# Key-side sums of linear attention: exponentials as the stationary operand, values with a column of ones as the moving one

## The chip, the cores and the metric

The kernel runs on one core of a Trainium2 chip. The metric is the device time of one execution in microseconds (us); the time before is the median of three runs, 832.02 us (829.52, 832.53 and 832.02). One further execution was recorded by the hardware profiler, and all rows below are from it.

The engines are named as the profile names them: PE is TensorE's matmul, PEld its weight load (the load of the stationary operand), DVE is VectorE, ACT is ScalarE, POOL is GpSimd and SP is SyncE, which issues nearly all DMAs here.

## The reference

Three stages follow each other. The first is linear attention over 4 batches, 8 heads, 576 tokens and head size 64; the change is in this stage alone.

```
proj = x @ w_phi                               # x is q or k, 64 -> 128 features
proj = proj - max(|proj|, over features)
phi(x) = [exp(proj), exp(-proj)]               # 256 features
kv  = sum over keys of phi(k)[f] * v[d]        # 256 x 64 per head
z   = sum over keys of phi(k)[f]               # 256 per head
out = (phi(q) @ kv) / (phi(q) @ z + 1e-6)
```

The second stage routes each token to one of 8 experts (two layers, 512 to 1024 to 512, with relu), the third is a gated feed-forward block with an RMS norm (512 to 1536 to 512). Their matmuls run in float32r, those of the attention in float32.

## The kernel before

The instructions are not written in the order in which they run. The code hands tasks to a planner (class `Graph`): each task has an engine, an estimated duration, its input and output buffers and a priority. The planner fills the engines' queues greedily: of the tasks whose inputs and buffers are there, it takes for an engine the one that can start first, and among equals the one with the lower priority number. The result is one fixed list for each engine, run in order.

For a batch b the function `attn` makes these tasks. Heads go in pairs; 512 of the 576 tokens ("main") are worked on pair by pair in four chunks of 128 (index c), and the 64 left over of all heads together (the pass "L"). The key passes come in the order pair 0, "L", pairs 1 to 3, with priorities b·100 + 0 to 4, the query passes after them from b·100 + 10 on. The experts' tasks of the batch have priorities from 1000 on, so they fill what the attention leaves.

- A pass loads its tokens (L417, L420), projects them on PE (L446, eight matmuls into one of two double banks named pq), takes the largest absolute value (L450, DVE) and subtracts it (L452, DVE, tile d). A bank is free again when the subtraction has read it.
- For keys, ACT makes both exponentials (L546, tile e; L539 for the left tokens, tile el).
- `kv_part` (L518) sums over the keys: the stationary operand is v of a chunk and head (128 keys x 64), the moving one both exponentials (128 keys x 256). The result lies with the 64 value columns on partitions, one head in each half of the partitions, ten matmuls a pair of heads (five chunks, the left tokens being the fifth).
- `sums` (L486) adds the exponentials of the chunks on DVE (L493; in batches 1 to 3 also L496 and L500), and `zn` (L504) finishes z on PE by matmuls with one moving column of ones (L515). In batch 0 there are 20 such matmuls a pair, in batches 1 to 3 eight.
- The sum over keys lies transposed to what the queries need. ACT copies it out of PSUM (L558, tile ks), and `ktr` (L561) has PE transpose both halves (L565) into the same bank beside z. DVE copies the bank out (L568, tile kv, 128 features x 2 heads x 2 halves x 65: 64 columns of kv and one of z).
- For queries, PE transposes d (L464, shown as L227), ACT makes the exponentials (L467, tile qp), and L613 multiplies: per head 16 matmuls of a stationary 128 x 64 (64 query tokens) with a moving 128 x 65 (kv and z). L580 does this for the left tokens. L475 to L479 divide on DVE; transposes and L624/L626 make the experts' input xh.

The host lays q, k and the left tokens out (`kernel`), v comes as it is.

Of the kernel before, what the change touches and what calls it, by code (L numbers as in the profile page):

```python
# [8 lines left out]
F32 = mybir.dt.float32  # L9
# [9 lines left out]
FE = 128  # L19
# [227 lines left out]
def dve(n, psum=False):  # L247
    return 0.13 + n / 960.0
# [6 lines left out]
class K:  # L255
# [123 lines left out]
    def attn_slots(self, ctx):  # L379
        g, p = self.g, self.pool(ctx, "at", side="left")  # L380
        self.attn_consts(p)
        mk = lambda *a: self.mk(p, *a)
        mk("qk", 6, [P, NC, P])
        mk("v", 3, [P, 2, NC, D])
        mk("vl", 2, [P, 2, NC, D])
        mk("d", 3, [P, 2, NC, FE])
        mk("e", 2, [P, 2 * NC, 2, FE])
        mk("el", 1, [P, NC, 2, FE])
        for _, _, a in g.slots["vl"]:
            self.nc.gpsimd.memset(a, 0.0)  # L390
        mk("es", 2, [P, 4, 2 * FE])
        mk("ks", 1, [P, 2 * FE])
        mk("qp", 2, [P, 2, NC, P])
        mk("qpl", 1, [P, 2, NC, P])
        mk("x", 2, [P, NC, P])
        mk("xl", 1, [P, 4 * D])
        mk("kv", 6, [P, 2, 2, D + 1])
        mk("m", 3, [P, 2 * NC])
        mk("r", 2, [P, NC])
        self.ones = p.tile([P, 1], F32, name="ones")  # L400
        self.nc.gpsimd.memset(self.ones, 1.0)
        self.halves = p.tile([P, 2], F32, name="halves")
        self.nc.gpsimd.memset(self.halves, 0.0)
        for j in range(2):
            self.nc.gpsimd.memset(self.halves[j * 64:j * 64 + 64, j:j + 1], 1.0)

    def attn(self, b, prio):

# [5 lines left out]
        def load(src, pr, np_):  # L414
            t = g.buf("qk")
            if pr != "L":
                g.t("SP", 0.5, lambda: nc.sync.dma_start(t.ap, src[b, pr].rearrange("p (c t) -> p c t", c=NC)),  # L417
                    w=[t], prio=np_, nbytes=2 * MAIN * D * 4)
            else:
                g.t(eng, 0.6, lambda: dma(t.ap, self.l[b].rearrange("p (c t) -> p c t", c=NC)),  # L420
                    w=[t], prio=-1 if b == 0 else np_, nbytes=2 * MAIN * D * 4)
            return t

        def load_v(pr, np_):
            if pr != "L":
                t = g.buf("v")
                g.t("SP", 0.5, lambda: nc.sync.dma_start(
                    t.ap, self.v[b, 2 * pr:2 * pr + 2, 0:MAIN].rearrange("h (p c) d -> p h c d", c=NC)),
                    w=[t], prio=np_ + (2.5 if b == 0 else 0), nbytes=2 * MAIN * D * 4)
                return t  # L430
            t = g.buf("vl")
            for j in range(2):
                g.t("SP", 0.6, lambda j=j: nc.sync.dma_start(
                    t.ap[j * 64:(j + 1) * 64, j], self.v[b, j::2, MAIN:S].rearrange("h t d -> t h d")),
                    w=[t], prio=np_ + (1.8 if b == 0 else 0), nbytes=LEFT * H * D * 2)
            return t

# [45 lines left out]
        kv, ready = {}, []  # L483
        el = vl = None

        def sums(pr, e, np_):  # L486


            es = g.buf("es")
            ev = lambda: e.ap.rearrange("p (j a k) f x -> p a j k (f x)", j=2, a=2)  # L490
            sv = lambda: es.ap.rearrange("p (j b) x -> p j b x", j=2)
            ex = lambda: el.ap[:, (pr % 2) * 2 + pr // 2].rearrange("p f x -> p (f x)")
            g.t("DVE", dve(1024), lambda: nc.vector.tensor_tensor(  # L493
                out=sv(), in0=ev()[:, 0], in1=ev()[:, 1], op=ALU.add), r=[e], w=[es], prio=np_)
            if b:
                g.t("DVE", dve(512), lambda: nc.vector.tensor_tensor(  # L496
                    out=sv()[:, :, 0], in0=sv()[:, :, 0], in1=sv()[:, :, 1], op=ALU.add), rw=[es], prio=np_)
                for j in range(2):
                    r = slice(j * 64, j * 64 + 64)
                    g.t("DVE", dve(256), lambda j=j, r=r: nc.vector.tensor_tensor(  # L500
                        out=sv()[r, j, 0], in0=sv()[r, j, 0], in1=ex()[r], op=ALU.add), r=[el], rw=[es], prio=np_)
            return es

        def zn(pr, es, pk):  # L504

            z = lambda x: pk.ap[x:x + 64, 0:4 * (D + 1)].rearrange("p (j f d) -> p j f d", j=2, f=2)[:, :, :, D]
            for f in range(2):
                todo = [] if b else [(lambda x, f=f: z(x)[:, :, f], el.ap[:, (pr % 2) * 2 + pr // 2, f], self.halves)]
                for j in range(2):
                    for i in range(1 if b else 2):  # L510
                        todo.append((lambda x, f=f, j=j: z(x)[:, j, f:f + 1], es.ap[:, 2 * j + i, f * FE:(f + 1) * FE],
                                     self.ones))
                for n, (o, w, m) in enumerate(todo):
                    for x in range(0, FE, 64):
                        nc.tensor.matmul(o(x), lhsT=w[:, x:x + 64], rhs=m, start=b > 0 or n == 0,  # L515
                                         stop=b > 0 or n == len(todo) - 1, skip_group_check=True)

        def kv_part(pr, e, v, np_, pk, part):  # L518


            def fn():
                for c in part:
                    for j in range(2):
                        v_, e_ = (v.ap[:, j, c], e.ap[:, j * NC + c]) if c < NC else (
                            vl.ap[:, j, pr], el.ap[:, (pr % 2) * 2 + pr // 2])
                        nc.tensor.matmul(pk.ap[j * 64:j * 64 + 64, 0:2 * FE], lhsT=v_,
                                         rhs=e_.rearrange("p f e -> p (f e)"), start=(c == 0), stop=(c == NC))
            g.t("PE", len(part) * 0.44 + 0.1, fn, r=([e, v] if 0 in part else []) + ([el, vl] if NC in part else []),
                rw=[pk], prio=np_)

        for i, pr in enumerate([0, "L", 1, 2, 3]):
            np_ = prio + i
            t = load(self.k, pr, np_)
            v = load_v(pr, np_)
            d = proj(t, np_)
            if pr == "L":
                el, vl, qpl = g.buf("el"), v, g.buf("qpl")
                for f in range(2):
                    g.t("ACT", act(512, False), lambda f=f, d=d: nc.scalar.activation(  # L539
                        el.ap[:, :, f].rearrange("p (h c) f -> p h c f", h=2), d.ap[:, :, 0:2], AF.Exp,  # L540
                        scale=1.0 - 2.0 * f), r=[d], w=[el], prio=np_)
                queries(d, lambda a, c: a[:, c % 2, 2 + c // 2], qpl, np_)
            else:
                e = g.buf("e")
                for f in range(2):
                    g.t("ACT", act(1024, False), lambda f=f, d=d, e=e: nc.scalar.activation(  # L546
                        e.ap[:, :, f], d.ap.rearrange("p h k f -> p (h k) f"), AF.Exp, scale=1.0 - 2.0 * f),
                        r=[d], w=[e], prio=np_)
                ready.append((pr, e, v, np_))
            if el is None:  # L550
                first = g.buf("pa")
                kv_part(*ready[0], first, range(NC))
                continue
            for pr, e, v, np_ in ready:
                pk, ks = first if pr == 0 else g.buf("pa"), g.buf("ks")
                es = sums(pr, e, np_)
                kv_part(pr, e, v, np_, pk, (NC,) if pr == 0 else range(NC + 1))
                g.t("ACT", act(256), lambda pk=pk, ks=ks: nc.scalar.copy(ks.ap, pk.ap[:, 0:2 * FE]),  # L558
                    r=[pk], w=[ks], prio=np_)

                def ktr(pr=pr, es=es, ks=ks, pk=pk):  # L561
                    zn(pr, es, pk)
                    o = pk.ap[:, 0:4 * (D + 1)].rearrange("p (j f d) -> p f j d", j=2, f=2)
                    for f in range(2):
                        nc.tensor.transpose(o[:, f, :, 0:D], ks.ap[:, f * FE:(f + 1) * FE], self.ident)  # L565
                g.t("PE", (0.9 if b else 1.3), ktr, r=[ks, es, el], rw=[pk], prio=np_)
                kv[pr] = g.buf("kv")
                g.t("DVE", dve(4 * (D + 1)), lambda pk=pk, o=kv[pr]: nc.vector.tensor_copy(  # L568
                    o.ap.rearrange("p j f d -> p (j f d)"), pk.ap[:, 0:4 * (D + 1)]), r=[pk], w=[kv[pr]], prio=np_)
            ready = []  # L570
# [763 lines left out]
```

## Time and profile before

| | |
|---|---|
| time, median of three runs | 832.02 us |
| the profiled execution | 829.16 us, its span 827.5 us |
| PE busy | 810.1 us, 98% of the span |
| DVE, ACT busy | 588.2 us, 399.7 us |
| mean granted TensorE clock | 0.995 of full speed |

The span is cut into three parts. The attention and the experts share the engines until some 395 us (the attention's last matmul starts at 270.8 us). In the stretch before 395 us the decoding of the third stage's weights begins on DVE and ACT; from 396 us on the third stage runs, whose matmuls are the largest groups of the page. A float32 matmul shows as two records, so a count of 16 is eight matmuls. Records of PE overlap, since a matmul's end is that of its last result; what a group of them costs is therefore read from its start to the start of the next group.

### The profile page before, as it was taken

Reading aid. Unit: us, or ns where it says so; the run is one execution under the profiler, and the core shown is the slowest. Engines: PE = TensorE matmul, PEld = TensorE weight load, DVE = VectorE, ACT = ScalarE, POOL = GpSimd, SP = SyncE. Lnnn points to the kernel's source line nnn. Section 1 sums busy time; section 2 is a strip of 40 time slices with the busy share of each in tenths; the row PEclk is TensorE's granted clock in tenths of the full one; section 3 lists DMA queues with packets and bytes.
Section 4 is the critical chain, followed back from the end, with each engine's and each line's share of the span. In section 5 each row is a group of like instructions: output and inputs, shape, how many; then the busy total and the mean of one; then the engine's idle time right before and its main releaser. Section 6 shows DMA issues by size and latency. Waiting matters only on the chain.

```text
span 827.5 us, 15957 instructions
## 1 busy us (share of the span) xinstructions
PE 810.1 (98%) x6552; PEld 745.3 (90%) x6553; DVE 588.2 (71%) x1041; ACT 399.7 (48%) x685; POOL 3.0 (0%) x20
## 2 busy tenths in 40 slices
PE   7989999999999999999799999999999999999997
PEld 6878898898989999999798999999999999999996
DVE  6697787777885459996699948898777554565533
ACT  4364363336534165451667545567354444454522
POOL 1000000000000000000000000000000000000000
PEclk9999999999999999999999999999999999999999
DMA  7354325424302555786537334553132223314102
GB/s 210 86 179 166 85 77 192 132 80 147 113 28 66 196 195 172 236 280 214 169 143 227 129 114 163 186 181 127 58 102 104 73 104 115 115 58 127 39 1 77
DMA packets 74560, 108.91 MB, mean 132 GB/s; under 512 B 10352, under 2 KB 55536, under 8 KB 73968
## 3 DMA queue, kind: packets, MB, share of 16 engines
q1 hardware_dynamic: 74176, 107.48, 39.5%
q8 instruction: 54, 0.88, 0.4%
q10 hardware_dynamic: 304, 0.33, 0.1%
q14 instruction: 26, 0.21, 0.1%
HBM read 73.11 MB, written 34.68 MB: 130 GB/s over the span
## 4 chain that ended last, share of the span: by engine, by line
PE 47%; ACT 2%; DVE 1%; issue 1%; DMA 0%; DVEq 0%; ACTq 0%
PE pz L1055 30%; PE pz L1101 17%; ACT w L934 0%; ACT L1080 0%; ACT fk L1061 0%; DMA out<-row 0%; DVE a L1093 0%; ACT row L870 0%; PE pz L1018 0%; ACT fk L1080 0%; DVE fk L1065 0%; DVE z L876 0%; DVE z L879 0%; DVE yu L973 0%; DVE fk L1088 0%
## 5 line engine op out<-in xcount | busy, mean ns | idle before, releaser
L1055 PE MATMUL pz<-xa,xh 128*128 128x384 f32 x798 | 151.4, 340 | 2.8 <-ACT fk L1061 2.1
L1055 PEld LDWEIGHTS pz<-xa,xh 128*128 128x128 f32 x798 | 141.7, 189 | 8.0 <-ACT fk L1061 3.0
L1055 PE MATMUL pz<-xa,w 128*128 128x384 f32 x714 | 133.9, 338 | 0.6 <-ACT fk L1061 0.6
L1055 PEld LDWEIGHTS pz<-xa,w 128*128 128x128 f32 x714 | 126.4, 188 | 4.6 <-ACT fk L1061 0.9
L1061 ACT ACTIVATE fk<-pz 128x384 f32<-128x384 f32 x144 | 70.6, 490 | 119.9 <-PE pz L1055 119.4
L1065 DVE TENSOR_TENSOR fk<-pz,fk 128x384 f32<-128x384 f32 x108 | 60.0, 555 | 93.0 <-PE pz L1055 53.5
L1101 PE MATMUL pz<-xh,a 128*128 128x512 f32 x342 | 87.1, 392 | 0.0
L1101 PE MATMUL pz<-w,a 128*128 128x512 f32 x306 | 78.8, 393 | 0.8 <-ACT a L1091 0.5
L761 PE MATMUL ph<-xh,w 128*128 128x288 f32 x528 | 77.0, 298 | 0.0
L761 PEld LDWEIGHTS ph<-xh,w 128*128 128x128 f32 x528 | 71.4, 188 | 2.4 <-issue 1.5
L1101 PEld LDWEIGHTS pz<-xh,a 128*128 128x128 f32 x342 | 63.4, 188 | 10.0 <-DVE a L1093 0.2
L770 PE MATMUL ph<-h,w 128*128 128x288 f32 x480 | 67.9, 296 | 0.0
L1101 PEld LDWEIGHTS pz<-w,a 128*128 128x128 f32 x306 | 56.6, 188 | 10.2 <-ACT a L1091 0.9
L770 PEld LDWEIGHTS ph<-h,w 128*128 128x128 f32 x480 | 64.5, 188 | 0.7 <-issue 0.4
L791 ACT CAST w<-wr 128x1024 fp32r<-128x1024 f32 x32 | 33.6, 1049 | 51.8 <-PE ps L770 14.4
L450 DVE TENSOR_REDUCE m<-pq 128x8 f32<-128x1024 f32 x36 | 43.7, 1219 | 14.7 <-PE pq L446 14.5
L1091 ACT CAST a<-fk 128x768 fp32r<-128x768 f32 x36 | 30.1, 836 | 43.8 <-DVE fk L1088 43.5
L467 ACT ACTIVATE qp<-ps 128x512 f32<-128x512 f32 x64 | 34.3, 603 | 31.4 <-PE ps L227 27.2
L1093 DVE TENSOR_TENSOR a<-fk,a 128x768 fp32r<-128x768 f32 x36 | 34.4, 955 | 18.9 <-ACT a L1091 18.9
L792 DVE TENSOR_TENSOR w<-wr,w 128x1024 fp32r<-128x1024 f32 x32 | 39.1, 1223 | 11.2 <-ACT w L791 11.0
L446 PE MATMUL pq<-wraw,qk 64*128 64x128 f32 x576 | 42.5, 287 | 3.8 <-DVE d L452 3.6
L446 PEld LDWEIGHTS pq<-wraw,qk 64*128 64x128 f32 x576 | 35.7, 190 | 9.1 <-DVE d L452 4.1
(190 smaller groups left out, 1168.7 us busy)
## 6 DMA issues: line engine op xcount, KB each, us to landing
wr<-in_moe_w SPq DMA_DIRECT2D x32, 512.0 KB, 3.7
z<-wdr SPq DMA_DIRECT2D x13, 896.0 KB, 4.6
xdr<-xh SPq DMA_DIRECT2D x4, 2304.0 KB, 8.7
wdr<-z SPq DMA_DIRECT2D x10, 896.0 KB, 4.6
yu<-ydr SPq DMA_DIRECT2D x8, 768.0 KB, 4.9
raw<-in_moe_w_val SPq DMA_DIRECT2D x12, 512.0 KB, 4.3
raw<-in_moe_w_gate SPq DMA_DIRECT2D x12, 512.0 KB, 4.5
raw<-in_moe_w_out SPq DMA_DIRECT2D x12, 512.0 KB, 3.9
```

Of the source, the lines that this page charges most:

```text
L446: nc.tensor.matmul(pp.ap[:, hf, k * FE:(k + 1) * FE], lhsT=t.ap[r, k], rhs=self.wraw[r], start=True, stop=True)
L450: g.t("DVE", dve(1024), lambda: nc.vector.tensor_reduce(out=m.ap, in_=pv(), axis=AX.X, op=ALU.max, apply_absolute_value=True), r=[pp], w=[ ...
L467: g.t("ACT", act(512), lambda f=f: nc.scalar.activation(qp.ap[:, f].rearrange("p c t -> p (c t)"), pd.ap, AF.Exp, scale=1.0 - 2.0 * f), r= ...
L761: self.nc.tensor.matmul(ph[:, 0:HS], lhsT=wv[:, a, c, fs], rhs=xh[:, x, c, cs], start=(c == 0 and i == 0), stop=(c == NC - 1 and i == 2))
L770: self.nc.tensor.matmul(ph[:, 0:HS], lhsT=wv[:, a, f], rhs=hs[f][:, x, cs], start=(f == 0 and i == 0), stop=(f == 7 and i == 2))
L791: g.t("ACT", act(1024, False), lambda: nc.scalar.copy(w.ap[:, 0], wr.ap), r=[wr], w=[w], prio=pr - AHEAD)
L792: g.t("DVE", dve(1024), lambda: nc.vector.tensor_tensor(out=w.ap[:, 1], in0=wr.ap, in1=w.ap[:, 0], op=ALU.subtract), r=[wr], rw=[w], prio= ...
L1055: nc.tensor.matmul(ps.ap[:, 0:UT], lhsT=flat(rec)[:, at:at + P], rhs=xa[op].ap[:, x, c], start=first and c == 0 and k == 0, stop=c == 1 an ...
L1061: g.t("ACT", act(UT), lambda: nc.scalar.activation(t.ap[:, h], ps.ap[:, 0:UT], fn), r=[ps], w=[d], use=[t], prio=pr - SOON)
L1065: g.t("DVE", dve(UT), lambda: nc.vector.tensor_tensor(out=t.ap[:, h], in0=ps.ap[:, 0:UT], in1=t.ap[:, h], op=ALU.add), r=[ps], w=w, rw=[d] ...
L1093: g.t("DVE", dve(n_), lambda a=a, vl=vl, hs=hs: nc.vector.tensor_tensor(out=a.ap[:, 1, hs], in0=vl.ap[:, hs], in1=a.ap[:, 0, hs], op=ALU.s ...
L1101: nc.tensor.matmul(po[3 * h + t].ap, lhsT=a.ap[:, x, h, t * P:(t + 1) * P], rhs=flat(rec)[:, at:at + DM], start=(n == 0 and k == 0 and not ...
```

## The change

The roles of the operands in the sum over keys are exchanged. The exponentials become the stationary operand, 64 of the 128 features at a time (the two calls write the two halves of the partitions), and the values with a column of ones behind them the moving one, 65 columns. The result then has the features on partitions and z as its 65th column, which is the layout that tile kv has. `sums`, `zn`, the copy ks and the transposes go. The tiles v and vl get a 65th column, set to one by POOL (in vl only for the rows of the own head); the host lays v out anew, so that a partition's part of it is in one piece in memory, and the left tokens' values lie beside l.

```diff
-        mk("v", 3, [P, 2, NC, D])
-        mk("vl", 2, [P, 2, NC, D])
+        mk("v", 3, [P, 2, NC, D + 1])
+        mk("vl", 2, [P, 2, NC, D + 1])
...
         for _, _, a in g.slots["vl"]:
             self.nc.gpsimd.memset(a, 0.0)
-        mk("es", 2, [P, 4, 2 * FE])
-        mk("ks", 1, [P, 2 * FE])
+            for j in range(2):
+                self.nc.gpsimd.memset(a[j * 64:j * 64 + 64, j, :, D:], 1.0)
+        for _, _, a in g.slots["v"]:
+            self.nc.gpsimd.memset(a[:, :, :, D:], 1.0)
...
-                    t.ap, self.v[b, 2 * pr:2 * pr + 2, 0:MAIN].rearrange("h (p c) d -> p h c d", c=NC)),
+                    t.ap[:, :, :, 0:D], self.v[b, pr].rearrange("p (h c d) -> p h c d", h=2, c=NC)),
...
-                    t.ap[j * 64:(j + 1) * 64, j], self.v[b, j::2, MAIN:S].rearrange("h t d -> t h d")),
+                    t.ap[j * 64:(j + 1) * 64, j, :, 0:D],
+                    self.l[b, j * 64:(j + 1) * 64, MAIN:].rearrange("t (h d) -> t h d", d=D)),
...
-                for c in part:
-                    for j in range(2):
-                        v_, e_ = (v.ap[:, j, c], e.ap[:, j * NC + c]) if c < NC else (
-                            vl.ap[:, j, pr], el.ap[:, (pr % 2) * 2 + pr // 2])
-                        nc.tensor.matmul(pk.ap[j * 64:j * 64 + 64, 0:2 * FE], lhsT=v_,
-                                         rhs=e_.rearrange("p f e -> p (f e)"), start=(c == 0), stop=(c == NC))
-            g.t("PE", len(part) * 0.44 + 0.1, fn, r=([e, v] if 0 in part else []) + ([el, vl] if NC in part else []),
+                for j in range(2):
+                    for f in range(2):
+                        at = (2 * j + f) * (D + 1)
+                        for c in part:
+                            v_, e_ = (v.ap[:, j, c], e.ap[:, j * NC + c, f]) if c < NC else (
+                                vl.ap[:, j, pr], el.ap[:, (pr % 2) * 2 + pr // 2, f])
+                            for x in range(0, FE, 64):
+                                nc.tensor.matmul(pk.ap[x:x + 64, at:at + D + 1], lhsT=e_[:, x:x + 64], rhs=v_,
+                                                 start=c == j == f == 0, stop=c == NC, skip_group_check=True)
+            g.t("PE", len(part) * 0.53 + 0.1, fn, r=([e, v] if 0 in part else []) + ([el, vl] if NC in part else []),
...
-                es = sums(pr, e, np_)
-                g.t("ACT", act(256), lambda pk=pk, ks=ks: nc.scalar.copy(ks.ap, pk.ap[:, 0:2 * FE]),
-                    r=[pk], w=[ks], prio=np_)
-
-                def ktr(pr=pr, es=es, ks=ks, pk=pk):
-                    zn(pr, es, pk)
...
-                g.t("PE", (0.9 if b else 1.3), ktr, r=[ks, es, el], rw=[pk], prio=np_)
```

The changed kernel has 640 matmuls of 64 x 65 (line L494 there) where 160 of 64 x 256, 176 with one or two moving columns and 32 transposes stood; 52 instructions of DVE and 16 of ACT go; all others are there in the same number. The planner orders the attention anew. From the first of three experts' groups in the last batch's attention on (PE's row 416 of before) PE's list is the same to the end of the program, and so are those of the other engines from about there.

PE in batch 0, before, from the first sum over keys (e, v: exponentials and values of a pair; el, vl: of the left tokens; ps: the PSUM banks; qk: tokens to be projected):

```order
L526 MATMUL ps_82<-e_166,v_158 64x256 x8
L446 MATMUL pq_85<-wraw,qk_156 128x128 x8
L227 MATMUL ps_83<-ident,d_165 128x128 x4
L526 MATMUL ps_82<-el_168,vl_161 64x256 x2
L526 MATMUL ps_84<-e_167,v_159 64x256 x8
...
L515 MATMUL ps_82<-ones,es_171 64x1 x8
L565 MATMUL ps_82<-ident,ks_173 128x2x64 x2
L446 MATMUL pq_89<-wraw,qk_157 128x128 x8
L446 MATMUL pq_85<-wraw,qk_152 128x128 x8
...
L526 MATMUL ps_81<-e_166,v_160 64x256 x8
...
L526 MATMUL ps_83<-e_167,v_158 64x256 x8
```

And now, from the same place:

```order
L494 MATMUL ps_82<-v_158,e_166 64x65 x32
L443 MATMUL pq_85<-wraw,qk_156 128x128 x8
L227 MATMUL ps_83<-ident,d_165 128x128 x4
L494 MATMUL ps_82<-vl_161,el_168 64x65 x8
L494 MATMUL ps_84<-v_159,e_167 64x65 x8
...
L494 MATMUL ps_81<-v_160,e_166 64x65 x8
...
L494 MATMUL ps_82<-v_158,e_167 64x65 x8
...
L443 MATMUL pq_89<-wraw,qk_157 128x128 x8
...
L443 MATMUL pq_85<-wraw,qk_152 128x128 x8
L443 MATMUL pq_89<-wraw,qk_153 128x128 x8
```

The projections qk_157 and qk_152, the first two of the queries in batch 0, stood between the sums of the second and the third pair; now they stand behind the sums of all four.

DVE in batch 0, before, from the first sum of exponentials on (m: largest values, d: differences, es: sums of exponentials, kv: the finished sums):

```order
L493 TENSOR_TENSOR es_171<-e_166 128x1024
L452 TENSOR_TENSOR d_165<-pq_85,m_188 128x1024
L493 TENSOR_TENSOR es_172<-e_167 128x1024
L450 TENSOR_REDUCE m_186<-pq_89 128x8
L450 TENSOR_REDUCE m_187<-pq_85 128x8
L452 TENSOR_TENSOR d_163<-pq_89,m_186 128x1024
L452 TENSOR_TENSOR d_164<-pq_85,m_187 128x1024
L568 COPY kv_180<-ps_82 128x260
...
L450 TENSOR_REDUCE m_188<-pq_89 128x8
L493 TENSOR_TENSOR es_172<-e_167 128x1024
L568 COPY kv_181<-ps_84 128x260
```

And now:

```order
L447 TENSOR_REDUCE m_190<-pq_89 128x8
L449 TENSOR_TENSOR d_165<-pq_85,m_192 128x1024
L449 TENSOR_TENSOR d_163<-pq_89,m_190 128x1024
L447 TENSOR_REDUCE m_191<-pq_85 128x8
L526 COPY kv_184<-ps_82 128x260
L449 TENSOR_TENSOR d_164<-pq_85,m_191 128x1024
L526 COPY kv_185<-ps_84 128x260
...
L526 COPY kv_186<-ps_81 128x260
L526 COPY kv_187<-ps_82 128x260
L447 TENSOR_REDUCE m_192<-pq_89 128x8
```

The last of these rows, the reduction of the first query pass, stood ahead of the copies of three pairs; now it stands behind all four.

## Rows read from the trace of the kernel before

**Rows 1.** The page's first part: busy time of each engine.
```profile
PE 810.1 (98%) x6552; PEld 745.3 (90%) x6553; DVE 588.2 (71%) x1041; ACT 399.7 (48%) x685; POOL 3.0 (0%) x20
```

**Rows 2.** Busy time by stretch: length, PE, PEld, DVE, ACT, POOL, clock, DMA share, GB/s.
```profile
23.00:67.00 44.00, 41.49 (x695) 33.78 (x691) 35.34 (x72) 21.12 (x38) 0.00 (x0) 1.00 0.53 166
67.00:248.00 181.00, 181.00 (x2249) 159.64 (x2246) 142.06 (x294) 80.14 (x144) 0.00 (x0) 1.00 0.32 105
248.00:394.00 146.00, 146.00 (x1206) 144.37 (x1205) 104.05 (x204) 63.04 (x108) 0.00 (x0) 1.00 0.59 193
```

**Rows 3.** PE in order of time, batches 1 and 3: start, us, line, operation, records.
```profile
81.71 1.95 PE L526 MATMUL ps<-e,v 128*64 128x256 f32 x16
...
84.02 1.85 PE L761 MATMUL ph<-xh,w 128*128 128x288 f32 x12
85.81 0.63 PE L515 MATMUL ps<-ones,es 128*64 128x1 f32 x16
...
86.74 1.16 PE L446 MATMUL pq<-wraw,qk 64*128 64x128 f32 x16
...
99.19 2.04 PE L613 MATMUL ps<-kv,qp 128*64 128x65 f32 x64
101.16 1.16 PE L446 MATMUL pq<-wraw,qk 64*128 64x128 f32 x16
...
230.19 1.95 PE L526 MATMUL ps<-e,v 128*64 128x256 f32 x16
...
232.40 0.58 PE L515 MATMUL ps<-ones,es 128*64 128x1 f32 x16
...
234.87 0.63 PE L515 MATMUL ps<-ones,es 128*64 128x1 f32 x16
...
235.71 1.04 PE L227 MATMUL ps<-ident,d 128*128 128x128 f32 x8
```

**Rows 4.** PE in order of time, batch 0.
```profile
12.51 2.85 PE L526 MATMUL ps<-e,v 128*64 128x256 f32 x16
15.29 1.16 PE L446 MATMUL pq<-wraw,qk 64*128 64x128 f32 x16
...
17.45 1.90 PE L526 MATMUL ps<-e,v 128*64 128x256 f32 x16
...
19.60 0.23 PE L515 MATMUL ps<-halves,el 128*64 128x2 f32 x4
...
21.18 2.06 PE L446 MATMUL pq<-wraw,qk 64*128 64x128 f32 x32
```

**Rows 5.** Granted clock (third number from the right) behind the first idle time.
```profile
12.50:14.20 1.70, 1.70 (x10) 1.00 (x10) 1.70 (x3) 0.95 (x1) 0.00 (x0) 0.50 0.94 275
```

**Rows 6.** Groups by line up to 420 us: busy us, mean ns of one, idle before.
```profile
L613 PE MATMUL ps<-kv,qp 128*64 128x65 f32 x1024 | 34.5, 223 | 0.8 <-ACT qp L467 0.8
L613 PEld LDWEIGHTS ps<-kv,qp 128*64 128x64 f32 x1024 | 31.7, 137 | 3.4 <-issue 2.2 <-ACT qp L467 1.0
L493 DVE TENSOR_TENSOR es<-e 128x1024 f32<-128x1024 f32 x16 | 19.5, 1218 | 1.7 <-ACT e L546 1.4 <-PE ps L515 0.2
L500 DVE TENSOR_TENSOR es<-es,el 64x256 f32<-64x256 f32 x24 | 10.0, 416 | 1.3 <-ACT el L539 0.9
L496 DVE TENSOR_TENSOR es<-es 128x512 f32<-128x512 f32 x12 | 8.2, 682 | 0.0
```

**Rows 7.** DVE in batch 0: the first query pass's reduction.
```profile
23.21 1.22 DVE L450 TENSOR_REDUCE m<-pq 128x8 f32<-128x1024 f32 x1
```

**Rows 8.** PE: the experts' first group, and where the common list begins.
```profile
67.20 3.44 PE L761 MATMUL ph<-xh,w 128*128 128x288 f32 x24
...
248.60 1.83 PE L761 MATMUL ph<-xh,w 128*128 128x288 f32 x12
```

**Rows 9.** DMA from 92 to 98 us in 40 slices: busy tenths, GB/s.
```profile
DMA  9998934359999844652000000000000000000000
GB/s 341 355 345 236 92 61 61 48 205 369 389 364 278 205 104 103 145 126 53 3 22 10 0 0 0 0 0 0 0 0 0 0 0 0 0 0 0 0 0 0
```

More of the change, by code (lines that the diff above doesn't have):

```diff
@@ L399, in attn_slots @@
         mk("r", 2, [P, NC])
[L400 to L403, printed above, removed]
-        for j in range(2):
-            self.nc.gpsimd.memset(self.halves[j * 64:j * 64 + 64, j:j + 1], 1.0)
     def attn(self, b, prio):
@@ L419, in load @@
             else:
-                g.t(eng, 0.6, lambda: dma(t.ap, self.l[b].rearrange("p (c t) -> p c t", c=NC)),
+                g.t(eng, 0.6, lambda: dma(t.ap, self.l[b, :, 0:MAIN].rearrange("p (c t) -> p c t", c=NC)),
                     w=[t], prio=-1 if b == 0 else np_, nbytes=2 * MAIN * D * 4)
@@ L484, in attn @@
         el = vl = None
[L486 to L516, printed above, removed]
@@ L518, in kv_part @@
         def kv_part(pr, e, v, np_, pk, part):
             def fn():
-                for c in part:
-                    for j in range(2):
-                        v_, e_ = (v.ap[:, j, c], e.ap[:, j * NC + c]) if c < NC else (
-                            vl.ap[:, j, pr], el.ap[:, (pr % 2) * 2 + pr // 2])
-                        nc.tensor.matmul(pk.ap[j * 64:j * 64 + 64, 0:2 * FE], lhsT=v_,
-                                         rhs=e_.rearrange("p f e -> p (f e)"), start=(c == 0), stop=(c == NC))
@@ L554, in attn @@
             for pr, e, v, np_ in ready:
-                pk, ks = first if pr == 0 else g.buf("pa"), g.buf("ks")
-                es = sums(pr, e, np_)
+                pk = first if pr == 0 else g.buf("pa")
                 kv_part(pr, e, v, np_, pk, (NC,) if pr == 0 else range(NC + 1))
-                g.t("ACT", act(256), lambda pk=pk, ks=ks: nc.scalar.copy(ks.ap, pk.ap[:, 0:2 * FE]),
-                    r=[pk], w=[ks], prio=np_)
-                def ktr(pr=pr, es=es, ks=ks, pk=pk):
-                    zn(pr, es, pk)
-                    o = pk.ap[:, 0:4 * (D + 1)].rearrange("p (j f d) -> p f j d", j=2, f=2)
-                    for f in range(2):
-                        nc.tensor.transpose(o[:, f, :, 0:D], ks.ap[:, f * FE:(f + 1) * FE], self.ident)
-                g.t("PE", (0.9 if b else 1.3), ktr, r=[ks, es, el], rw=[pk], prio=np_)
                 kv[pr] = g.buf("kv")
@@ L1320 @@
     a = np.stack([inputs[n][:, :, MAIN:].reshape(B, 2, 2, 2, LEFT, D) for n in "kq"])
-    lay["l"] = a.transpose(1, 3, 6, 0, 2, 4, 5).reshape(B, P, MAIN)
+    a = a.transpose(1, 3, 6, 0, 2, 4, 5).reshape(B, P, MAIN)
+    v = inputs["v"][:, :, MAIN:].reshape(B, NC, 2, LEFT, D).transpose(0, 2, 3, 1, 4).reshape(B, P, NC * D)
+    lay["l"] = np.concatenate([a, v], axis=2)
+    v = inputs["v"][:, :, :MAIN].reshape(B, NC, 2, P, NC, D)
+    lay["v"] = v.transpose(0, 1, 3, 2, 4, 5).reshape(B, NC, P, MAIN)
     for name in _INS:
```

## The prediction

> **What bounds the kernel now.** I read the page's first part first: PE is busy 98% of the span and DVE 71% [rows 1]. A mean over stages with different limits proves little, so the next view is the busy time by stretch [rows 2]. From 67 to 248 us PE is busy 181.00 of 181 us, from 248 to 394 us 146.00 of 146, while DVE has 142 and 104. In these two stretches the experts' matmuls stand ready to fill whatever the attention leaves, so each microsecond of PE that the attention no longer needs should come off the time. From 23 to 67 us it is different: PE is busy 41.49 of 44 us and DVE 35.34; the experts of batch 0 cannot start before its attention is done (their first group starts at 67.20 [rows 8]), so there the chain through PE, DVE and ACT counts, not one engine. From 248.60 us on PE's list is the same in both kernels, so what is gained has to be gained by then, and everything behind it is shifted as a whole.
>
> **The change on PE.** The old sum costs, read from start to start, for the second pair of batch 0: 2.15 us for the ten matmuls (17.45 to 19.60) and 1.58 us for 20 matmuls of the ones and two transposes (19.60 to 21.18), together 3.73 [rows 4]. The first pair has 2.78 (12.51 to 15.29) plus 0.43 for its left tokens (a fifth of the second pair's 2.15) and the same 1.58, so 4.8. Batch 0: 4.8 + 3 x 3.73 = 16.0 us. In batches 1 to 3 a pair costs 2.31 + 0.93 = 3.24 us for the second third of the way (81.71 to 84.02, 85.81 to 86.74) and 2.21 + 0.84 = 3.05 us for the last (230.19 to 232.40, 234.87 to 235.71) [rows 3]; I take the middle, 3.15, times twelve: 37.8 us. Removed in all: 53.8 us.
>
> The new form needs no guess, since the queries' product has it already: a stationary 128 x 64, a moving 128 x 65 in float32, the two halves of the partitions by turns. Its 64 records from 99.19 to 101.16 are 32 matmuls in 1.97 us, 61.6 ns each [rows 3]. A pair has 4 x 5 x 2 = 40 of them: 2.46 us. Twelve pairs are 29.5 us; batch 0 has 4 x 2.46 = 9.9 plus 0.85, since the granted clock is 0.50, the 1.2 GHz level, from 12.50 to 14.20 [rows 5] and half of those 1.7 us is lost to the first sum as it was to the old one. Added: 40.2 us. Saved on PE: 8.3 us in batches 1 to 3 and 5.3 in batch 0, 13.6 in all.
>
> **What the sum rests on, and a rule against it.** In the form that I borrow the loads seem to be hidden: each lasts 137 ns, yet PEld's busy time for 1,024 of them is 31.7 us, 31 ns each, and PE's is 34.5 [rows 6], so several are under way at once beside the matmuls. The Trainium skill has a rule that speaks against this (TensorE: Matmul & The Clock Gate, Part 3: Packing small matmuls): a weight load overlaps matmuls in flight only where the row group differs. Here both halves use all 128 rows and differ in columns alone, so by that rule load and matmul would add up, and a change that makes 640 loads where there were 368 would lose: the sum would be the third rival's 883 us, against 819 by the row of the queries' product. That row is of this very form, so the rule gets a small chance.
>
> **DVE and ACT.** The sums of exponentials go: 19.5 + 10.0 + 8.2 = 37.7 us of DVE [rows 6]; on ACT the 16 copies. From 67 us on that is idle time on engines that are not the bottleneck and counts for nothing. In batch 0 it counts, and there the new order takes something back. PE's list now has all four sums one behind the other, and the queries' first projection behind them. Walked through: the first sum from 12.5 as before, 14 matmuls until 14.2 and 18 more, to 15.3; a projection 1.1 (1.16 with its last result's delay [rows 3, 4]) and four transposes 0.6 (eight take 1.04 [rows 3]); the remaining 128 matmuls at 61.6 ns, 7.9; the projection 1.1: it ends at 26.0. Its reduction on DVE starts at about 26.1 and not at 23.21 [rows 7], 2.9 us late. From there on DVE has less to do until the experts start: three sums of 1.22 us, two of 0.68 and three of 0.42 (one of batch 0, the others of the first two pairs of batch 1) are 6.3 us [rows 6], and three copies of the finished sums, 260 columns and so about 0.43 each (256 take 0.416), 1.3 us, are done before. If the chain stays as tight as it is, the experts start 6.3 + 1.3 - 2.9 = 4.7 us earlier, at 62.5. The bounds: the freed DVE time turns into idle time and only the delay is left, 2.9 us late; or PE alone decides, then 5.3 + 2 x 0.69 - 0.84 (the second pair's old tail, which stands behind 67.20) = 5.8, and with the 2.5 us of PE's idle time in this stretch 8.3 us early. I take 4.7, which is nearer to the PE sum. Behind 67.20 follow that 0.84 and ten pairs at 0.69: 7.7 us.
>
> **Smaller edits.** v now lands in pieces of 256 bytes instead of one per head of 1 KB, 16 loads of 256 KB. The only pieces of that size in the rows are the old vl: about 95.0 us the engines moved 104, 103, 145, 126 and 53 GB/s at 8, 4, 4, 6 and 5 tenths busy, where they had moved 369 at nine tenths with longer pieces just before [rows 9]. That is about half the rate, so a load of v takes about 0.6 us more. Three stand in the first microseconds, ahead of key loads whose projections wait for DVE anyway; later ones are issued many microseconds before their use. I take nothing, with 0 and 1 us as bounds. POOL's column of ones (seven small memsets for four that go) ends before the first sum at 12.5; nothing. No wait is added but one: the left queries' product follows the fourth sum with one projection between, 1.1 us for a copy of 0.43 on DVE, which has nothing else then.
>
> **The sum.** 4.7 + 7.7 = 12.4 us against the profiled execution's 829.16 us: 816.8. The three timed runs lie 2.2 us above that execution in the mean (831.36), so I say 819.0.
>
> **Rivals.**
> 1. Batch 0 gives nothing or takes back: the queries are held up behind four sums, DVE is idle from some 20 to 26 us, and the time that it saves comes where ACT's exponentials or PE's order decide. For it: DVE is idle 8.7 of 44 us there already [rows 2], so it is no tight bound. Against it: a third less DVE work in the keys' passes. Gain 7.7 down to 7.7 - 2.9 = 4.8: 823.7 to 826.6.
> 2. PE decides in batch 0 too and part of its idle time vanishes: gain 13.6 to 16.1, 815 to 817.8 on the timed scale less what the idle time gives, at best 813.5.
> 3. Slower: the loads do not hide. The place is each of the 640 matmuls. Where nothing longer than one column moves, 16 records of loads and products and two transposes take 0.93 us, 52 ns a record [rows 3]; if such a time came on top of the 31 ns of streaming, a matmul would cost 166 ns, 106 us in all, 52 more than now: 883. It decides from 84 ns a matmul on (53.8 us over 640). Against it stand all 1,024 records of the same form.
> 4. The saving is hidden: the stretch up to 394 us is set by decoding the third stage's weights and not by PE, and the time stays at about 831. Against it: DVE has 104 of 146 us, PE has no gap, and the decoding starts when the attention ends, which is earlier too.
>
> **How the numbers follow.** The forecast has 0.57, the first rival 0.20, the second 0.10, the fourth 0.08, the slow one 0.05. The range takes in the forecast and rivals 1 and 2, 813.5 to 826.5; the likeliest case alone has 816 to 822. About 0.5%, 4.2 us, is what a measurement of this kernel tells from no change, so faster means below 827.9: 0.87; the same 0.08; slower 0.05.
>
> **What would show it.** Right: the new matmuls at 61 to 63 ns from start to start in groups of 40; the experts' first group at 62 to 63 us; the group that is at 248.60 now at 235 to 237 us; the same distance as before from there to the end; DVE's busy time down by 37 to 38 us. The batch-0 step fails if the first group of the experts comes later than 64 us, with PE waiting for DVE's subtractions between 28 and 50 us. The price fails if a group of 40 takes over 2.7 us. The whole is wrong if the distance from that common group to the end grows.

## The result and the profile after

The changed kernel takes 821.47 us (median of four runs, 819.36 to 822.14), the kernel before in the same series 831.6 us: ratio 0.9877, 95% interval 0.986 to 0.9894. Two later series timed it again, at 819.89 us (0.9867, 0.9845 to 0.989) and 818.8 us (0.985, 0.9826 to 0.9875). The forecast was 819.0 us. One execution in each of the two series with whole blocks (experiment 5) fell in a slower state of the chip and is left out of their times. The profiled execution takes 819.36 us with a span of 817.7, 9.8 us less than before.

The page's first part, which answers to [rows 1]:

```profile
PE 798.4 (98%) x7128; PEld 748.5 (92%) x7129; DVE 554.4 (68%) x989; ACT 394.5 (48%) x669; POOL 3.2 (0%) x23
```

PE's share is what it was, in a shorter span: its busy time fell by 11.7 us, DVE's by 33.8. The busy time by stretch, with the borders at the same places of the program as in [rows 2]:

```profile
23.00:65.00 42.00, 39.38 (x757) 34.96 (x751) 31.66 (x66) 20.73 (x36) 0.00 (x0) 1.00 0.60 179
65.00:238.00 173.00, 173.00 (x2636) 160.70 (x2635) 115.76 (x247) 75.46 (x133) 0.00 (x0) 1.00 0.34 106
238.00:384.00 146.00, 145.23 (x1197) 143.36 (x1195) 103.09 (x206) 62.96 (x108) 0.00 (x0) 1.00 0.61 196
```

The middle stretch is shorter by 8 us and PE still has no gap in it, while DVE lost 26 us there. In the first one PE's idle time is 2.6 us where it was 2.5, though DVE has less to do: what that stretch lost is PE's own work. The new sums, PE in order of time (start, us, line, operation, records), in batch 0 and in batch 1 (answers to [rows 3, 4]):

```profile
18.00 0.64 PE L494 MATMUL ps<-v,e 128*64 128x65 f32 x16
...
20.33 0.64 PE L494 MATMUL ps<-v,e 128*64 128x65 f32 x16
...
67.98 0.69 PE L494 MATMUL ps<-v,e 128*64 128x65 f32 x16
...
70.46 0.39 PE L675 MATMUL ps<-g,mean 128*128 128x8 f32 x2
```

From 18.00 to 20.33 are 40 matmuls (80 records with those of the left tokens between), 58.3 ns each. A pair that stands alone among other work takes 2.48 us (67.98 to 70.46), with the change from another kind of matmul. Read in this way over the whole program, the sums and all that belonged to them took 54.3 us before (without one wait of 0.34 us) and take 40.5 us now. Where the program has got to, PE again; first after, then before, whose first two places are in [rows 8]:

```profile
61.73 3.44 PE L719 MATMUL ph<-xh,w 128*128 128x288 f32 x24
...
242.15 1.75 PE L728 MATMUL ph<-h,w 128*128 128x288 f32 x12
...
379.86 3.36 PE L728 MATMUL ps<-h,w 128*128 128x288 f32 x24
...
389.59 6.03 PE L1013 MATMUL pz<-xa,xh 128*128 128x384 f32 x24 [0.78 <-ACT row L928]
```

```profile
253.44 1.75 PE L770 MATMUL ph<-h,w 128*128 128x288 f32 x12
...
391.17 3.36 PE L770 MATMUL ps<-h,w 128*128 128x288 f32 x24
...
400.89 4.67 PE L1055 MATMUL pz<-xa,xh 128*128 128x384 f32 x24 [0.57 <-ACT row L970]
```

The experts' first group starts 5.5 us earlier (61.73 against 67.20 [rows 8]), the first group of the second expert matrix of batch 3 is 11.3 us earlier, the last one too, and at the end 9.8 are left. So 5.8 us come between the first two places, and 1.5 go again behind the third: the 24 records of the third stage's first long run take 6.03 us where they took 4.67. The clock shows why (stretch, length, busy times; the granted clock is the third number from the right):

```profile
12.00:14.00 2.00, 2.00 (x29) 1.78 (x28) 1.32 (x2) 1.88 (x2) 0.00 (x0) 0.50 0.94 245
...
390.00:392.00 2.00, 2.00 (x9) 2.00 (x8) 1.58 (x4) 2.00 (x3) 0.00 (x0) 0.55 1.05 395
392.00:394.00 2.00, 2.00 (x9) 2.00 (x8) 2.00 (x4) 0.75 (x3) 0.00 (x0) 0.60 0.63 229
```

From 390 to 394 us the granted clock is 0.55 to 0.60, close to the 1.2 GHz level, with PE busy all the time; in the eight microseconds before it PE was busy for 3.7. DVE in batch 0, the start of the first query reduction (answers to [rows 7]):

```profile
20.55 0.43 DVE L526 COPY kv<-ps 128x260 f32<-128x260 f32 x1 [0.77 <-PE ps L494]
...
22.88 0.43 DVE L526 COPY kv<-ps 128x260 f32<-128x260 f32 x1 [1.54 <-PE ps L494]
...
25.22 0.43 DVE L526 COPY kv<-ps 128x260 f32<-128x260 f32 x1 [1.91 <-PE ps L494]
26.31 1.22 DVE L447 TENSOR_REDUCE m<-pq 128x8 f32<-128x1024 f32 x1 [0.66 <-PE pq L443]
```

It starts at 26.31, 3.1 us later than before, and DVE idles 4.9 us in these four waits for PE's sums.

### The profile page after: what moved, and what is told of

The parts are those of the page before. It is cut to its first block, busy times and chain, and to the rows that moved or that the text cites. A ratio compares the mean times of both kernels' runs of the same rounds, so it can differ in the third digit from the quotient of the medians.

```text
span 817.7 us, 17027 instructions
## 1 busy us (share of the span) xinstructions
PE 798.4 (98%) x7128; PEld 748.5 (92%) x7129; DVE 554.4 (68%) x989; ACT 394.5 (48%) x669; POOL 3.2 (0%) x23
## 4 chain that ended last, share of the span: by engine, by line
PE 48%; ACT 2%; DVE 1%; issue 1%; DMA 0%; DVEq 0%; ACTq 0%
PE pz L1013 31%; PE pz L1059 17%; ACT L1038 0%; ACT fk L1019 0%; DMA out<-row 0%; DVE a L1051 0%; ACT w L892 0%; ACT row L828 0%; PE pz L976 0%; ACT fk L1038 0%; DVE fk L1023 0%; DVE z L834 0%; DVE z L837 0%; DVE yu L931 0%; DVE fk L1046 0%
## 5 line engine op out<-in xcount | busy, mean ns | idle before, releaser
L447 DVE TENSOR_REDUCE m<-pq 128x8 f32<-128x1024 f32 x36 | 43.8, 1220 | 28.7 <-PE pq L443 28.5
```

What stands on the lines that cost most here:

```text
L447: g.t("DVE", dve(1024), lambda: nc.vector.tensor_reduce(out=m.ap, in_=pv(), axis=AX.X, op=ALU.max, apply_absolute_value=True), r=[pp], w=[ ...
```

## The experiments

**1. The DVE sums put back.** The changed kernel with the old additions of exponentials into a tile that nothing reads.

```diff
+        mk("es", 2, [P, 4, 2 * FE])
...
                 kv_part(pr, e, v, ...)
+                sums(pr, e, np_)
```

> The changed kernel with the sums of exponentials put back on DVE (16 of 1.22 us, 12 of 0.68, 24 of 0.42: 37.7 us), which nothing reads. Theory A (PE's shorter sum makes the gain, DVE counts in batch 0 alone): the fill stretch from 65 to 238 us keeps its length within 1 us, the experts' first group comes 1 to 5 us later than 61.73, time 822 to 826 us. Rival B (what DVE no longer does makes the gain): most of the 10 us is given back, 828 to 832 us.

Measured: 820.45 us, ratio 0.9857 (0.9836 to 0.9878): below both forecasts and as fast as without them (818.8 to 821.47 in three series). Page and PE in order of time:

```profile
PE 799.4 (98%) x7128; PEld 748.0 (91%) x7129; DVE 587.5 (72%) x1041; ACT 395.4 (48%) x669; POOL 3.2 (0%) x23
```

```profile
62.03 0.69 PE L513 MATMUL ps<-v,e 128*64 128x65 f32 x16
...
64.51 3.44 PE L739 MATMUL ph<-xh,w 128*128 128x288 f32 x24
...
380.73 3.36 PE L748 MATMUL ps<-h,w 128*128 128x288 f32 x24
```

DVE has its 33 us again, the experts start 2.8 us later (64.51), and the last expert group is only 0.9 us later. PE was not idle for it: a later sum (62.03) now stands ahead of the experts instead of behind. When the experts start is a place in PE's list, not a gain or a loss.

**2. Only the DVE sums taken away.** The kernel before, with z read from single chunks; it leaves most keys out of z.

```diff
-                es = sums(pr, e, np_)
+                es = e
```

> The kernel before without the sums of exponentials on DVE; the matmuls with the ones read single chunks of the exponentials in their place, so z lacks most keys. PE and ACT do what they did. Theory A: only batch 0's chain gets shorter, 0 to 5 us, time 826 to 832 us, with PE without a gap from 67 to 248 us and a distance from the experts' first group to the common list as before (181 us within 1). Rival B: 820 to 824 us.

Measured: 833.34 us against 831.81, ratio 1.0016 (1.0003 to 1.0029): not faster.

```profile
PE 813.6 (98%) x6552; PEld 748.2 (90%) x6553; DVE 555.2 (67%) x989; ACT 400.2 (48%) x685; POOL 3.0 (0%) x20
```

33 us of DVE gone and nothing gained. The order moved here too, and the experts' first group starts at 72.54 instead of 67.20 us, with no loss to match. With experiment 1 this shows from both sides that the gain does not come from DVE, in batch 0 either. ACT's 16 copies were not put back by themselves; but the version of experiment 4 leaves out the copies and DVE's sums alike, has dearer matmuls, and takes 834 us.

**3. The queries between the sums.** In batch 0 the sums of pairs 2 and 3 come behind two more query projections. The planner also orders anew what follows: up to some 220 us PE's groups come in another order than in the changed kernel.

```diff
-                rw=[pk], prio=np_)
+                rw=[pk], prio=10.5 if b == 0 and pr in (2, 3) else np_)
```

> The changed kernel with one number changed: in batch 0 the sums of pairs 2 and 3 get the priority 10.5, so that the first two query projections stand on PE between the sums of pairs 1 and 2, as in the kernel before. Theory A (the delay of DVE's query work behind four sums costs part of batch 0's gain): the reduction of the first query pass starts near 21.5 us and not 26.3, the experts' first group 1 to 3 us before 61.73, time 818.5 to 820.5 us. Rival C (ACT's exponentials or PE's order set that chain): the first group within 0.5 us of 61.73, time 821.5 within 1 us.

Measured: 818.39 us, ratio 0.9833 (0.981 to 0.9856). The first query reduction on DVE, and the experts' first group on PE:

```profile
22.36 1.22 DVE L447 TENSOR_REDUCE m<-pq 128x8 f32<-128x1024 f32 x1 [0.56 <-PE pq L443]
...
62.24 1.86 PE L719 MATMUL ph<-xh,w 128*128 128x288 f32 x12
```

The reduction starts 3.9 us earlier than in the changed kernel (26.31), the experts do not (61.73). The time was 3 us under the changed kernel's first series, so both ran again in one series:

> The order with the last two query features ahead of the sums of pairs 2 and 3, once more, now beside the changed kernel in one series. Theory 1 (the sums delay the first batch's last query reductions, and PE waits for what follows): 1 to 3 us below the changed kernel of the same series. Theory 2 (TensorE's waits in the first batch only move; the 3 us between the two earlier series are scatter): within 1 us of it, both at 818 to 821 us.

> The changed kernel as it is, a third time, beside the order run. Theory 1: 819 to 822 us, 1 to 3 us above the order run. Theory 2: 818 to 821 us, within 1 us of it; in either, the span follows where the low granted clock falls: 814.9 us when it falls on no long run of matmuls, 817.7 us when it falls on the first sums and on the 24 matmuls of the last stage.

Measured: 818.57 us (0.984, 0.9814 to 0.9865) and 818.8 us for the changed kernel (0.985, 0.9826 to 0.9875). The order makes no difference that can be told; the 3 us were scatter between series. No version tried is shown to beat the changed kernel. The profiled execution of the changed kernel in this series (span 817.0 us), PE in order of time:

```profile
62.37 3.44 PE L719 MATMUL ph<-xh,w 128*128 128x288 f32 x24
...
380.50 3.36 PE L728 MATMUL ps<-h,w 128*128 128x288 f32 x24
...
390.21 4.50 PE L1013 MATMUL pz<-xa,xh 128*128 128x384 f32 x24 [0.78 <-ACT row L928]
```

It fits neither of the two spans that were forecast: the 24 records run at full clock, yet the experts start 0.6 us later than in the first execution. Why they do was not followed up.

**4. The halves kept apart.** The same 640 matmuls, but first the five of one half and then the five of the other.

```diff
-                        for c in part:
...
-                            for x in range(0, FE, 64):
+                        for x in range(0, FE, 64):
+                            for c in part:
```

> The changed kernel with the loop over the two halves of the features outside the one over the chunks: four or five matmuls into one half of the partitions follow each other, then those of the other half. Same instructions, same buffers. Theory S (the two halves run side by side, each matmul alone lasts twice 58 ns): 640 matmuls at 117 ns, 37 us more, about 855 us where PE is full. Rival P (loads and matmuls are pipelined alike whichever half they write): 58 ns as now, 821.5 us within 1. If the loads of one half no longer hide, more than 117 ns.

Measured: 834.19 us, ratio 1.0024 (1.0006 to 1.0042). PE in order of time, the page's first part below:

```profile
87.30 0.73 PE L494 MATMUL ps<-v,e 128*64 128x65 f32 x10
...
87.94 0.51 PE L494 MATMUL ps<-v,e 128*64 128x65 f32 x7
...
88.28 0.22 PE L494 MATMUL ps<-v,e 128*64 128x65 f32 x1
88.28 0.22 PE L494 MATMUL ps<-vl,el 128*64 128x65 f32 x1
88.34 0.51 PE L494 MATMUL ps<-v,e 128*64 128x65 f32 x7
...
89.97 0.51 PE L494 MATMUL ps<-v,e 128*64 128x65 f32 x7
...
90.88 1.09 PE L227 MATMUL ps<-ident,d 128*128 128x128 f32 x8
```

```profile
PE 813.9 (98%) x7128; PEld 763.8 (92%) x7129; DVE 554.7 (67%) x989; ACT 394.7 (47%) x669; POOL 3.2 (0%) x23
```

The step from 87.94 to 88.34 is the five matmuls of a half; from 87.94 to 89.97 there are five such steps, 81 ns a matmul. 640 x (81 - 58.3) = 14.5 us more. Over the whole program the sums take 55.4 us from start to start, 14.9 more than in the changed kernel; PE's busy time is 15.5 us above the first execution, the time 12.7 to 15.4 above the three series. The whole gain of the change hangs on the alternation of halves. Neither theory's number came out, but the single records say that Theory S had the mechanism. In the changed kernel they start in twos, 6 or 7 ns apart (18.642 and 18.649, 18.700 and 18.707 us), and a new two every 58 ns: both halves run side by side. Here a record stands alone, some 58 ns behind the one before it (53 to 61), except where the half changes: there records of both halves start together (88.28, left tokens of one half and the first chunk of the other). Three of a step's ten records do, so a step is seven times 58 ns, 0.406 us, and a matmul takes 81 ns and not 117.

**5. Whole blocks.** One stationary block of 128 features, 320 matmuls.

```diff
-                            for x in range(0, FE, 64):
-                                nc.tensor.matmul(pk.ap[x:x + 64, at:at + D + 1], lhsT=e_[:, x:x + 64], rhs=v_,
+                            nc.tensor.matmul(pk.ap[:, at:at + D + 1], lhsT=e_, rhs=v_,
```

> Each pair of 64-wide stationary halves becomes one stationary block of 128 features: 320 matmuls in place of 640, each with 65 columns moving. Theory A (a weight load is hidden only behind a matmul on other columns of the array; loads to the same columns show): as with the halves kept apart, where a record took 40.5 ns in place of 29.2, so 13.5 ns of a 64-wide load stood beside 27 ns of columns; a 128-wide one would show 27 ns, a matmul of two records takes 108 ns, 320 x 108 = 34.6 us against 37.3 now, 2.8 us less, about 818 us. Theory B (loads are hidden in any case): 58 ns x 320 = 18.7 us, 18.7 us less, about 802 us. Theory C (a whole load shows in full, as with the 128x128 transposes, about 110 ns a record): 220 x 320 = 70 us, 33 us more, about 853 us.

Measured: 848.56 us (five executions, 848.25 to 856.65), ratio 1.0232 (1.0195 to 1.0268). PE in order of time and the page:

```profile
64.88 1.06 PE L493 MATMUL ps<-v,e 128*128 128x65 f32 x8
...
66.00 1.06 PE L493 MATMUL ps<-v,e 128*128 128x65 f32 x8
...
67.11 1.06 PE L493 MATMUL ps<-v,e 128*128 128x65 f32 x8
```

```profile
PE 828.4 (98%) x6488; PEld 780.9 (92%) x6489; DVE 554.6 (66%) x989; ACT 395.2 (47%) x669; POOL 3.2 (0%) x23
```

Ten matmuls from 64.88 to 67.11, 223 ns each: half as many matmuls, each nearly four times as long. Theory C had 220. Theory A had worked from 40.5 ns a record, which is a mean of lone records and twos. 71 us in place of 37 would be 34 more; from start to start the sums take 71.5 us, 31 more than the 40.5 of the changed kernel, and the time grew by 28.7 against the repeated run below. With the order of experiment 3 as well, the result is the same:

> Both edits together: the first batch's sums of pairs 2 and 3 put behind the last two query features, and whole 128-wide blocks. By Theory A 818 - 3 = 815 to 817 us, by B 799 to 801 us, by C 850 us; the part of the order is then seen as the difference from the run with blocks alone, 0.5 to 3 us.

Measured: 848.73 us, ratio 1.0214 (1.0193 to 1.0235). The order adds nothing here either.

**6. The same kernel again.** No edit; the question is the 1.5 us behind the last expert group.

> The changed kernel as it is, once more, beside the other kernels of this series. Theory 1 (the 1.5 us that went missing behind the last experts' group are a stretch of low granted clock that falls on 24 matmuls in this program): 820 to 822 us, and the 24 matmuls again take about 6.0 us. Theory 2 (where the low stretch falls is chance): 819 to 822 us, with the 24 matmuls anywhere from 4.5 to 6.0 us.

Measured: 819.89 us (816.5 to 821.32); the profiled execution is the fastest, with a span of 814.9. PE in order of time, then the clock:

```profile
60.22 3.44 PE L719 MATMUL ph<-xh,w 128*128 128x288 f32 x24
...
378.35 3.36 PE L728 MATMUL ps<-h,w 128*128 128x288 f32 x24
...
388.05 4.50 PE L1013 MATMUL pz<-xa,xh 128*128 128x384 f32 x24 [0.57 <-ACT row L928]
```

```profile
12.00:14.00 2.00, 1.84 (x64) 1.70 (x60) 2.00 (x2) 1.41 (x2) 0.00 (x0) 1.00 1.02 266
...
384.00:388.00 4.00, 3.03 (x11) 2.26 (x9) 2.55 (x5) 2.54 (x5) 0.00 (x0) 0.60 0.24 41
388.00:390.00 2.00, 1.95 (x11) 1.95 (x12) 2.00 (x5) 2.00 (x5) 0.00 (x0) 1.00 1.06 396
```

The clock falls here while PE waits for part of the time (384 to 388, busy 3.03 of 4 us), and the 24 records run at full clock in 4.50 us. At the start it does not fall at all between 12 and 14 us, and the experts start 1.5 us earlier. The clock is not all of that; PE's first projections, in the first execution and in this one:

```profile
4.54 0.48 PE L443 MATMUL pq<-wraw,qk 64*128 64x128 f32 x2 [0.30 <-DMA wraw<-in_w_phi]
5.27 2.05 PE L443 MATMUL pq<-wraw,qk 64*128 64x128 f32 x30 [0.25 <-DMA wraw<-in_w_phi]
```

```profile
4.17 2.67 PE L443 MATMUL pq<-wraw,qk 64*128 64x128 f32 x32
```

They end 0.5 us earlier here (6.84 against 7.32), since PE does not wait for the weights; the other 1.0 us comes from the second projections and the first sum. From the last expert group to the end it is 436.6 us here (814.9 - 378.35), 437.8 in the first execution, 436.5 in the third execution (817.0 - 380.50), 436.3 before (827.5 - 391.17). The kernel before is not spared either: in the version of experiment 2 the same 24 records take 6.03 us.

```profile
403.95 6.03 PE L1055 MATMUL pz<-xa,xh 128*128 128x384 f32 x24 [0.79 <-ACT row L970]
```

So the 1.5 us are where the low stretch happened to fall, and no cost of the change: theory 2.

**7. The gaps filled.** Eight matmuls that nothing reads, at the start of the third stage. This version leaves out part of that stage's result; its other work is unchanged.

```diff
+                    for _ in range(5 if keep and n == op == 0 and first else 0):
+                        self.fill(ps)
...
+                g.t("PE", 0.8, lambda pr=pr: [self.fill(pr) for _ in range(3)], r=[sp], ...
...
+        self.nc.tensor.matmul(ps.ap[:, UT:UT + P], lhsT=self.mean, rhs=self.mean, ...
```

> Eight matmuls that nothing reads (five behind the first product of the last stage, three behind the second spread of the row scales) fill the gaps of 1.7 us in which TensorE waits at the start of the last stage; they write free columns of the same banks. Theory 1 (the gaps are what lets the granted clock fall on the next 24 matmuls): these take 4.5 to 4.7 us in place of 6.0, the time is 1.0 to 1.5 us below the changed kernel of this series. Theory 2 (the low stretch comes whatever stands in the gaps): 24 matmuls at 6.0 us again, no gain, or up to 0.5 us more for the added work.

Measured: 819.51 us, ratio 0.9862 (0.9839 to 0.9885), against 819.89 for the same kernel without them.

```profile
387.08 1.27 PE L988 MATMUL pz<-mean 128*128 128x128 f32 x10
...
390.62 4.50 PE L1021 MATMUL pz<-xa,xh 128*128 128x384 f32 x24 [0.57 <-ACT row L929]
```

The 24 records take 4.50 us, but so they do without the filling in experiment 6. Whether filled gaps hold the clock up can't be told from this; that they bring no time can.

## Why the prediction was right

**The price.** I took 61.6 ns from the queries' product and it is 58.3 ns in a long run, 2.48 us a pair elsewhere against 2.46. Over the whole program the sums cost 54.3 us before (53.8 worked out) and 40.5 now (40.2), 13.8 us less against 13.6. PE's busy time fell by 11.7 us in the first execution and by 13.3 in the second (796.8 us), where the low clock fell on less work. This term carries the result. The product of keys and values itself got no cheaper (2.33 to 2.48 us a pair against 2.15 to 2.31 in [rows 3, 4]); what is saved are the matmuls of the ones and the transposes, 1.58 us a pair in batch 0 and 0.84 to 0.93 behind it. And the loads that I called hidden are in truth two halves side by side, each load taking its time, as experiment 4 shows; the borrowed row had this too, its records start in twos, 10 ns apart. The third rival's 166 ns for a matmul of 64 columns appear in no version; but the point from which the change loses, 84 ns, was well placed: kept in one half a matmul costs 81, and there the time is about that of before, 834 against 832 us. The fourth rival is out, since the stretch up to 394 us moved forward with PE.

**Batch 0: a right size for a wrong reason.** The query reduction came at 26.31 (26.1 forecast), and the experts at 61.73, 60.22 and 62.37 us in the three profiled executions (62.5 forecast). But my 4.7 us were DVE work that goes, less a delay on DVE, and that step failed: with all this work put back the time is the same, and without it the kernel before is no faster. What moved the experts is PE's own saving, with PE's idle time as it was (2.6 against 2.5 us); I had it as the upper bound of this term, 5.8 us, and as the second rival. That the number came out is luck. DVE's wait for the four sums (4.9 us, as the first rival had it) shows no cost either, since a version with the reduction at 22.36 is no faster. The sign that I had set for this step, experts later than 64 us, could not tell the two reasons apart. And the place scatters by 2.2 us between executions of one kernel, so the 5.5 us of the first are uncertain by as much.

**Behind the experts' start: 5.8 us, not 7.7.** From there to the first group of the second expert matrix of batch 3 PE's starts give the sums and all that belonged to them 32.48 us before and 25.16 after: 7.3 less, close to the 7.7 worked out. But the other groups together take 1.5 us more, up to 0.4 per kind (the queries' product 20.22 to 20.65). I had left them unchanged. The list is cut differently around the new groups, and a group behind another kind may begin with a dearer record; that this is the cause was not tested. The difference was the same 5.8 us in all three executions (318.13 us from the experts' first group to the last, 323.97 before).

**The distance to the end.** It was to stay, and grew by 1.5 us in the first execution; in the second and the third by 0.2. By the test that I had set, the first would have made the whole wrong, so one execution was too few for it.

**Other signs that missed.** The common group came at about 237.4 us (the second half of the 24 records from 235.77) where 235 to 237 were forecast. DVE's busy time fell by 33.8 us and not by 37 to 38: the rows that go do add up to 37.7, but DVE's records overlap (all its groups before add up to 639.4 us where the page has 588.2), and the page counts such time once. The lower bound of 813.5 is no sum of its terms: the second rival's 16.1 us, with PE's idle time already in them, give 815.3.

**Smaller edits.** Loads of v were to take 0.6 us more, from a rate that I read off by one slice in [rows 9]: the 104, 103, 145, 126 and 53 GB/s stand under 4, 4, 6, 5 and 2 tenths, about six tenths of the full rate and not half, which by the same working makes 0.4 us. The page of DMA issues, median from issue to landing, before and after:

```profile
v<-in_v SPq DMA_DIRECT2D x16, 256.0 KB, 2.9
```

```profile
v<-in_v SPq DMA_DIRECT2D x16, 256.0 KB, 3.4
```

It is 0.5, and since PE has no gap from 65 to 238 us, nothing waits for it there.

**The sum.** 12.4 us were forecast; the three series have 10.1, 11.9 and 12.6 us between their medians. Part of the agreement is luck, since the one term is too small for its place (4.8 to 7.0 us in the three executions, 4.7 forecast) and the other too large (5.8, 7.7 forecast). The fall of 9.8 in the first profiled execution is that sum less the 1.5 us of clock and some 2 us less behind the experts' start, plus 0.8 more in front of it.

## What to carry to other kernels

Where an engine stands at 98% with work always ready, count its own busy time before and after; a start that comes earlier or later may only be another order of the list. Price a new matmul by a row of exactly its form, including which columns of the array follow each other: the same work cost 58 or 81 ns per 64 columns of stationary data by that order alone, and 112 in blocks of 128 (half of 223). Look at the starts of single records too: a mean of 40 ns hid lone records and twos. Before a microsecond behind a change is explained, profile the same kernel twice.

## What the runs showed of the hardware

Two float32 matmuls that write different halves of the partitions run side by side. With the halves by turns records start in twos, 6 or 7 ns apart, and a two takes 58 ns (64 columns loaded and 65 moved in each record). With the same half five times in a row a lone record takes some 58 ns too, with a whole 128-wide block 111.5 ns. So in all three 64 columns take 56 to 58 ns, and only by turns do the two halves take them at once. The pace goes with the columns loaded and not with those moved, as long as few move: with one moving column (the old sums of the ones, 85.9 to 86.3 us) the twos also come every 58 ns, and the 128x128 transposes, which add to nothing, come every 109 ns (36.93 to 37.95 in the first execution). With 256 moving columns, in the old sums over keys (17.6 to 19.5 us), a two takes 216 ns. A load's own record lasts 137 to 140 ns in either order of the halves, so its length says nothing of the pace.

The Trainium skill's rule from the prediction (TensorE: Matmul & The Clock Gate, Part 3: Packing small matmuls) lets a load overlap matmuls in flight only where the row group differs. Here all rows are the same, and loads and matmuls of the two column halves start 7 ns apart, so its "only" does not hold for these records; the section also names a load into a background weight buffer as a second way, which no run here can show. The same page (LDWEIGHTS (loading the stationary operand)) has a load at its number of columns divided by 1.2 in ns; worked out from that, an estimate, 64 columns take 53 and 128 take 107. The pace of the records agrees, with 58 and 111.5 ns.

The granted clock of one and the same program falls at different places: at 390 to 394 us in one execution under busy matmuls, at 384 to 388 in another between waits. That moves the way from the last expert group to the end by 1.3 us (437.8 and 436.6). The spans of these two executions differ by 2.8 us (817.7 and 814.9); of the rest, about 1.0 us lies where the clock was low at the start, and 0.5 is the wait for the weights of the first projections.
